# An attention-then-MLP kernel on one core: the list scheduler orders the same instructions by its timeline simulation instead of its core simulation

## The chip, the cores and the metric

The kernel runs on one core of a Trainium2 chip. The core has five engines that run side by side, each with its own instruction queue, executed strictly in the order in which the queue was written: TensorE (PE, matrix products, with a separate loader for weights, PEld), VectorE (DVE), ScalarE (ACT), GpSimd (POOL) and SyncE (SP, which here issues all the transfers). Engines wait for one another by semaphores. The metric is the device time of one execution in microseconds (us); smaller is better.

## The reference

Four batches of 12,480 tokens with 128 channels go through an attention by way of 32 inducing points, and then through an MLP with a squared ReLU:

```python
def mab(q, kv):
    s = scale * (q @ kv.transpose(0, 2, 1))
    a = np.exp(s - s.max(-1, keepdims=True))
    a /= a.sum(-1, keepdims=True) + 1e-09
    return a @ kv
h = mab(I, x)                 # (4, 32, 128): the inducing points attend to the tokens
y = mab(x, h)                 # (4, 12480, 128): the tokens attend to h
r = np.maximum(y.reshape(49920, 128) @ w_in, 0.0)      # w_in 128 x 2048
out = (r * r) @ w_out                                  # w_out 2048 x 128
```

## The kernel before

**Stages.** For each batch the kernel does four things.

- `first(b)`: the scores of the inducing points against the tokens (matmul s, L236, seven groups of up to 1920 tokens), their largest value (L254), the exponential on ACT (L300), a transpose on DVE (en, L310), and 28 pieces of the product with x accumulated in PSUM (hacc, L323) and added up (hq, L331). At the end stand hs (L336), hn (L340), ht (L343) and hT (L346), which is h of this batch, transposed. On the way DVE finds the largest magnitude of x per group (xm, L292, 128 x 1920).
- `prepare(b)`: a chain of small steps that turns h and the weights into this batch's constants. Since a token's attention weights over the 32 points add up to one, the MLP is rewritten as a quadratic form in those weights. The chain is hwv (L448), maxima (L463 to L479), a broadcast (bc, L482, and two, L484), scalings, hwS (L520), R (L529), pl (L537), rb (L560), cat (L578), w4 (L596), and then four times: DVE builds a tile G of products (L605, four instructions of 128 x 512; L607 once), PE multiplies it by w_out (wq, L611, 16 matmuls), and the result is written to the weights w16. G has one buffer, so that the next G waits for the wq before.
- `second(b, G)`: the attention of the tokens to h in seven groups of four chunks (s, L236; e, L362 to L375; the result goes out to DRAM as ad, L389, and comes back in another layout as dT, L409). `squares(b, G)` adds rows to dT (sq, L422; z, L428; zz, L432 on POOL; a transfer, L434).
- The chunks: 26 per batch, 104 in all, of 480 tokens. A chunk has two **ups** (`Chunk.up`, L639: two matmuls into hp, a tile of two PSUM banks, of which there are two), two **lifts** (`Chunk.lift`, L648: ACT squares hp into g, 128 x 960; three buffers of g), and a **down** (`Chunk.down`: four matmuls L654 with w16 and one L655 with lin into po, two buffers; then o, L658 on ACT or L660 on DVE, three buffers; then a transfer of o out, L661).

**What sets the order.** The code gives the instructions in one order: for each chunk n, the lift of half j, the up of half j of chunk n+1, and after the first half the down of chunk n-1; behind each half `background` gives some steps of the next groups' `second` and `squares` and of the next batch's `first` and `prepare`. This is the order in which the code is written, not the one that runs. `tile.TileContext` holds a list scheduler: it takes the instructions as they were given, keeps what depends on what, simulates the engines with a model of how long each instruction takes, and writes each engine's queue in the order in which the instructions became ready and were picked in that simulation. It chooses no other instructions and no other buffer sizes. A few places are tied by hand, with `tc.issue_after` (what stands in it comes behind the instruction that is named).

```python
    for n, chunk in enumerate(chunks):
        ...
        for j in (0, 1):
            chunk.lift(j)
            if nxt:
                nxt.up(j)
            if j == 0 and n:
                chunks[n - 1].down()
            k += 1
            background(k)
```

**The start.** Before any chunk, DVE splits the two weight matrices, which arrive as 64-bit words, into parts that it can compute with (`narrow`, L206 to L212, for w_in, seven instructions for each of four pieces wi; the same for w_out), works through a block of small constants (fold, rep, slot, late, cut, pairs, singles: L80 to L135), and does `first(0)`. wo_m (L186) and wo_b (L189) belong to the preparation of w_out; behind them PE does the hwv of batch 0.

At the very end of the program stands a branch for inputs on which the quadratic form isn't exact enough; it isn't taken here and costs the branch alone.

## Time and profile before

| | us |
|---|---|
| Three runs | 576.62, 576.66, 575.87; median 576.62 |
| The profiled execution: span, which is its own time | 577.3 |
| PE busy (in the span) | 438.9 (76%) |
| DVE busy | 365.3 (63%) |
| ACT busy | 296.8 (51%) |
| POOL busy | 83.4 (14%) |
| All transfers: 100.82 MB | 175 GB/s in the mean |

The profile page gives, for one execution, the busy time of each engine, the span in 40 equal slices with a digit for the busy share, the granted clock of TensorE in the same slices, and the chain of work that ended last. In the rows of a timeline stand the start in us, the duration in us, the engine, the line of the kernel, the operation, output<-input with shapes, and the count; in brackets what the engine waited for ahead of it. The rows of a waits view read: engine, line <- engine and line waited for, then us in total, times, the longest. The rows of a windows view read: window, its length, then busy us (and count) of PE, PEld, DVE, ACT, POOL, then the granted clock, the share of the DMA engines and GB/s.

The profiled span is 0.7 us above the median of the runs.

### The profile page before, as it was taken

What the parts mean: (1) busy time and instruction counts of PE and PEld (TensorE: products, weight loads), DVE (VectorE), ACT (ScalarE), POOL (GpSimd) and SP (SyncE); (2) the same over time, 40 slices, a digit from 0 to 9 for tenths busy, and PEclk for the clock granted to TensorE, in tenths of its full rate; (3) what the DMA queues carried; (4) which work ended last, traced back from release to release, by engine and by line L of the source; (5) the groups of instructions that cost most, each with busy time, mean ns of one, the idle gap of its engine ahead of it and who ended that gap; (6) DMA issues with size and microseconds to landing.
All of it is one profiled execution on the core that took longest, in us unless ns stands there. A gap on an engine that the chain in (4) does not pass through costs nothing.

```text
span 577.3 us, 8820 instructions
## 1 busy us (share of the span) xinstructions
PE 438.9 (76%) x3083; PEld 204.5 (35%) x3083; DVE 365.3 (63%) x947; ACT 296.8 (51%) x419; POOL 83.4 (14%) x93
## 2 busy tenths in 40 slices
PE   1615465777798889769878899769777999897882
PEld 0014334522233536413333545313243555223330
DVE  6999758662555268997254298985534378767342
ACT  0030112437577266747875376628574476565771
POOL 0000011030211010242021021222011022422010
PEclk9999655997789569989889799969969599899997
DMA  8958715024528606565867535735866332334543
GB/s 322 399 214 277 277 69 154 1 86 155 179 80 305 199 20 226 172 182 167 280 226 230 178 102 186 270 104 145 311 211 190 107 105 72 97 126 130 168 132 131
DMA packets 64590, 100.82 MB, mean 175 GB/s; under 512 B 22800, under 2 KB 53776, under 8 KB 64528
## 3 DMA queue, kind: packets, MB, share of 16 engines
q1 hardware_dynamic: 64528, 100.08, 52.1%
q8 instruction: 28, 0.46, 0.3%
q14 instruction: 34, 0.28, 0.2%
HBM read 64.91 MB, written 31.95 MB: 168 GB/s over the span
## 4 chain that ended last, share of the span: by engine, by line
PE 44%; DVE 28%; ACT 13%; issue 6%; DMA 3%; POOL 3%; SPq 1%; POOLq 0%; ACTq 0%; DVEq 0%
PE po L654 10%; PE hp L639 9%; ACT g L648 8%; PE s L236 7%; DVE xm L292 5%; PE hwv L448 5%; PE hacc L323 4%; DVE G L605 3%; DMA outT_dram<-o 2%; PE po L655 2%; PE wq L611 2%; ACT o L658 2%; DVE e L362 2%; PE R L529 2%; DVE z L372 2%
## 5 line engine op out<-in xcount | busy, mean ns | idle before, releaser
L648 ACT ACTIVATE g<-hp 128x960 f16<-128x960 f32 x208 | 193.2, 970 | 87.9 <-PE hp L639 48.9
L639 PE MATMUL hp<-dT,pairs 96*128 96x480 f16 x416 | 122.0, 385 | 29.0 <-ACT g L648 28.1
L654 PE MATMUL po<-g,w 128*128 128x480 f16 x416 | 119.4, 399 | 16.1 <-ACT o L658 6.0
L368 POOL TENSOR_TENSOR e<-e,mx 128x480 f32<-128x480 f32 (+1 forms) x28 | 26.5, 947 | 334.8 <-DVE mx L364 222.8
L639 PEld LDWEIGHTS <-pairs 96*128 96x128 f16 x416 | 37.8, 99 | 97.6 <-issue 75.7
L654 PEld LDWEIGHTS <-w 128*128 128x128 f16 x416 | 41.1, 104 | 75.4 <-issue 43.9
L292 DVE TENSOR_REDUCE xm<-xp_False 128x1 f32<-128x1920 f32 (+1 forms) x28 | 55.7, 1989 | 5.3 <-DMA xp_False<-xT_dram 5.3
L658 ACT ACTIVATE o<-po,bias,osc 128x480 f32<-128x480 f32 x66 | 48.9, 753 | 18.9 <-PE po L655 7.1
L236 PE MATMUL s<-xp_False,indT_sb 128*32 128x480 f32 (+1 forms) x224 | 37.7, 743 | 20.5 <-DMA xp_False<-xT_dram 12.3
L323 PE MATMUL hacc<-xnb,en 128*32 128x128 f32 x784 | 39.2, 328 | 17.2 <-issue 9.3
L655 PE MATMUL po<-dT,lin 128*128 128x480 f16 x104 | 42.3, 408 | 2.7 <-DMA dT<-zz 2.7
L432 POOL TENSOR_TENSOR zz<-z 128x480 f16<-128x480 f32 (+1 forms) x28 | 28.9, 1030 | 87.8 <-DVE z L428 72.1
L660 DVE TENSOR_SCALAR o<-po,osc,bias 128x480 f32<-128x480 f32 x38 | 28.7, 767 | 18.0 <-DMA outT_dram<-o 6.8
L323 PEld LDWEIGHTS hacc<-xnb,en 128*32 128x32 f32 x784 | 26.7, 129 | 34.3 <-issue 20.1
L300 ACT ACTIVATE sT<-sT,nb 128x480 f32<-128x480 f32 (+1 forms) x28 | 18.2, 653 | 35.5 <-DVE nb L287 35.5
L236 PE MATMUL s<-xp_False,hT 128*32 128x480 f32 (+1 forms) x224 | 34.5, 628 | 2.1 <-DVE s L357 1.7
L375 POOL TENSOR_TENSOR e<-e,z 128x480 f32<-128x480 f32 (+1 forms) x28 | 27.6, 986 | 53.8 <-DVE z L374 48.6
L428 DVE TENSOR_SCALAR z<-sq,off,cut 128x480 f32<-128x480 f32 (+1 forms) x28 | 21.4, 764 | 21.8 <-PE sq L422 21.7
L605 DVE TENSOR_TENSOR G<-hwp,hw 128x512 f16<-128x512 f16 x64 | 30.1, 510 | 5.0 <-PE wq L611 4.7
L369 ACT ACTIVATE e<-e 128x480 f32<-128x480 f32 (+1 forms) x28 | 16.1, 574 | 31.6 <-POOL e L368 31.6
L362 DVE STREAM_TRANSPOSE e<-s 128x480 f32<-128x480 f32 (+1 forms) x28 | 18.0, 644 | 15.4 <-PE s L236 14.9
L331 DVE TENSOR_TENSOR hq<-hacc,hq 128x128 f32<-128x128 f32 x24 | 6.8, 284 | 33.0 <-PE hacc L323 33.0
(208 smaller groups left out, 498.6 us busy)
## 6 DMA issues: line engine op xcount, KB each, us to landing
outT_dram<-o SPq DMA_DIRECT2D x104, 240.0 KB, 2.2
xp_False<-xT_dram SPq DMA_DIRECT2D x24, 960.0 KB, 5.8
xnb<-xn_dram SPq DMA_DIRECT2D x28, 448.0 KB, 6.1
xnb<-xn_dram SPq DMA_DIRECT2D x24, 512.0 KB, 5.8
dT<-ad SPq DMA_DIRECT2D x72, 120.0 KB, 2.7
ad<-a SPq DMA_DIRECT2D x24, 240.0 KB, 2.7
dT<-zz SPq DMA_DIRECT2D x104, 30.0 KB, 1.9
wi<-w_in_dram SPq DMA_DIRECT2D x4, 512.0 KB, 5.4
```

The costliest lines, as they stand in the source:

```text
L236: nc.tensor.matmul(ps[32 * q:32 * q + 32, 0:w], lhsT, xp[:, w * q:w * q + w], start=True, stop=True,)
L292: nc.vector.tensor_reduce(st.xm[:, G:G + 1], st.xp[G], axis=AX.X, op=ALU.max, apply_absolute_value=True,)
L323: st.last = nc.tensor.matmul(hacc[32 * q:32 * q + 32, 0:P], en[:, t], xg[:, t % 8], start=t < 4, stop=t + 4 >= nb32,)
L362: nc.vector.transpose(ef[:, 0:wb], ps[:, 0:wb])
L432: nc.gpsimd.tensor_tensor(g[rows], zv[rows], zv[rows], op=ALU.mult)
L448: nc.tensor.matmul(ps[:, k * (MI + 1):(k + 1) * (MI + 1)], w_in_sb[:, f:f + P], st.hT[:, 96:P + 1], start=True, stop=True,)
L605: tt(g[:, :, MI * j:MI * j + n], hwp[:, :, 0:n], hw16f[:, :, s0:s0 + n], op=ALU.mult)
L639: nc.tensor.matmul(hp[:, i, 0:CH].rearrange("p (q t) -> p q t", q=4), pairs[0:96, (2 * j + i) * P:(2 * j + i + 1) * P], self.dT[0:96], sta ...
L648: nc.scalar.activation(self.g[:, 2 * j:2 * j + 2], self.hp.pop(j)[:, 0:2, 0:CH], AF.Square)
L654: nc.tensor.matmul(po[:, 0:CH], st.w16[:, i], self.g[:, i], start=i == 0, stop=False)
L655: nc.tensor.matmul(po[:, 0:CH].rearrange("p (q t) -> p q t", q=4), st.lin, self.dT, start=False, stop=True)
L658: nc.scalar.activation(o, po[:, 0:CH], AF.Identity, bias=st.bias, scale=st.osc)
```

## The change

One argument of the tile context is added. The scheduler then runs its timeline simulation, in place of the default core simulation, to decide which instruction of those that are ready comes next on each engine.

```diff
-    with tile.TileContext(nc) as tc:
+    with tile.TileContext(nc, schedule_with_timeline_sim=True) as tc:
         attend_then_relu2_mlp(tc, *aps)
```

Every engine gets the same instructions as before; what moves is their order, on PE, DVE, ACT, POOL and SP alike, and with it where each waits. Three places are shown. In the rows stand the line, the operation and output<-input with a running number, and x for a repetition.

**DVE at the start.** ni0 and ni1 are the first two pieces of w_in being narrowed, out of the words wi0 and wi1; the rows on fold to singles are the block of small constants. Before:

```order
L563 MEMSET cat_0_686 32x16
L206 TENSOR_SCALAR ni0_a_193<-wi0_171 128x512
L207 SCALAR_TENSOR_TENSOR ni0_a_193<-wi0_171,ni0_a_193 128x512
...
L206 TENSOR_SCALAR ni1_a_203<-wi1_173 128x512
L212 SCALAR_TENSOR_TENSOR w_in_sb_128<-ni0_m_194,ni0_r_195 128x512
L80 TENSOR_REDUCE fold_84<-ident_74 128x32 x2
L82 COPY rep_87<-fold_84 128x128
...
L135 CAST singles1_149<-fold_84 64x16
L207 SCALAR_TENSOR_TENSOR ni1_a_203<-wi1_173,ni1_a_203 128x512
```

And now:

```order
L563 MEMSET cat_0_686 32x16
L80 TENSOR_REDUCE fold_84<-ident_74 128x32 x2
L93 TENSOR_REDUCE late_97<-ident_74 128x1
L82 COPY rep_87<-fold_84 128x128
...
L135 CAST singles1_149<-fold_84 64x16
L206 TENSOR_SCALAR ni0_a_193<-wi0_171 128x512
L207 SCALAR_TENSOR_TENSOR ni0_a_193<-wi0_171,ni0_a_193 128x512
...
L206 TENSOR_SCALAR ni1_a_203<-wi1_173 128x512
L212 SCALAR_TENSOR_TENSOR w_in_sb_128<-ni0_m_194,ni0_r_195 128x512
L207 SCALAR_TENSOR_TENSOR ni1_a_203<-wi1_173,ni1_a_203 128x512
```

The block from fold to singles has moved from behind the first piece to ahead of it, and so ahead of DVE's first wait for wi0.

**PE among the chunks.** hp_3_20_0 is the first half's up of chunk 20 of the last batch, po_3_19 the down of chunk 19. Each matmul has a row for the loading of its weights ahead of it, left out here, as are repetitions. Before:

```order
L639 MATMUL hp_3_20_0_5295<-dT_3_5_5106,pairs_109 128x480
...
L639 MATMUL hp_3_20_1_5308<-dT_3_5_5106,pairs_109 128x480
...
L655 MATMUL po_3_17_5280<-dT_3_4_4995,lin1_147 128x480
...
L655 MATMUL po_3_18_5298<-dT_3_4_4995,lin1_147 128x480
...
L639 MATMUL hp_3_21_0_5313<-dT_3_5_5106,pairs_109 128x480
...
L655 MATMUL po_3_19_5316<-dT_3_4_4995,lin1_147 128x480
```

And now:

```order
L639 MATMUL hp_3_20_0_5295<-dT_3_5_5106,pairs_109 128x480
...
L654 MATMUL po_3_19_5316<-g_3_19_5293,w16_1_146 128x480
...
L639 MATMUL hp_3_20_1_5308<-dT_3_5_5106,pairs_109 128x480
...
L654 MATMUL po_3_19_5316<-g_3_19_5293,w16_1_146 128x480
...
L655 MATMUL po_3_19_5316<-dT_3_4_4995,lin1_147 128x480
...
L639 MATMUL hp_3_21_0_5313<-dT_3_5_5106,pairs_109 128x480
```

Before, two ups in a row were followed by two whole downs in a row, and the ups ran up to four chunks ahead of the downs (2.8 in the mean over the program). Now one up (two matmuls) and half a down (two matmuls) alternate here, and the ups are 1.5 chunks ahead. The alternation stands in chunks 8 to 17 of the first and of the second batch, 8 to 21 of the third and 16 to 25 of the last; over the program the ups are 2.1 chunks ahead in the mean.

**PE at the end of a batch.** R_1, rb_1, w4_1 and wq_1 are steps of the preparation of batch 1, hp_0_24 and hp_0_25 the last ups of batch 0, and po_0_22 to po_0_25 its last downs, of which the last row of each is shown. Before:

```order
L529 MATMUL R_1_1763<-wo_sb_129,hwS_1_1740 32x128 x16
...
L639 MATMUL hp_0_24_0_2110<-dT_0_6_1634,pairs_109 128x480
...
L596 MATMUL w4_1_1876<-w_hi_130,g4_1_1800 32x128
...
L655 MATMUL po_0_22_2113<-dT_0_5_1404,lin0_136 128x480
...
L611 MATMUL wq_1_0_1928<-w_hi_130,G_1_0_1919 128x128
...
L655 MATMUL po_0_23_2141<-dT_0_5_1404,lin0_136 128x480
...
L611 MATMUL wq_1_1_1975<-w_hi_130,G_1_1_1947 128x128
...
L639 MATMUL hp_1_0_0_2178<-dT_1_0_1914,pairs_109 128x480
...
L611 MATMUL wq_1_3_2076<-w_hi_130,G_1_3_2051 128x128
```

And now:

```order
L639 MATMUL hp_0_24_0_2110<-dT_0_6_1634,pairs_109 128x480
...
L529 MATMUL R_1_1763<-wo_sb_129,hwS_1_1740 32x128 x16
...
L655 MATMUL po_0_22_2113<-dT_0_5_1404,lin0_136 128x480
...
L655 MATMUL po_0_23_2141<-dT_0_5_1404,lin0_136 128x480
...
L639 MATMUL hp_1_0_0_2178<-dT_1_0_1914,pairs_109 128x480
...
L596 MATMUL w4_1_1876<-w_hi_130,g4_1_1800 32x128
...
L611 MATMUL wq_1_0_1928<-w_hi_130,G_1_0_1919 128x128
...
L611 MATMUL wq_1_1_1975<-w_hi_130,G_1_1_1947 128x128
...
L611 MATMUL wq_1_3_2076<-w_hi_130,G_1_3_2051 128x128
```

The steps of the preparation have moved back against the chunks. Counted in chunks whose ups and downs stand ahead on PE (a half is one of two ups, or some of the matmuls of a down), R moves from (23, 20) to (25.5, 22), rb from (24, 22) to (26, 25.5), wq_0 from (24.75, 23) to (28, 26) and wq_3 from (28, 26) to (30, 26.75); the ends of the second and third batch read alike.

## The prediction, made before the changed kernel was run

> **What bounds the kernel now.** First the page: span, busy times, the strips of 40 slices (14.4 us each) and the chain that ended last.
>
> ```profile
> span 577.3 us, 8820 instructions
> PE 438.9 (76%) x3083; PEld 204.5 (35%) x3083; DVE 365.3 (63%) x947; ACT 296.8 (51%) x419; POOL 83.4 (14%) x93
> PE   1615465777798889769878899769777999897882
> DVE  6999758662555268997254298985534378767342
> ACT  0030112437577266747875376628574476565771
> PEclk9999655997789569989889799969969599899997
> PE 44%; DVE 28%; ACT 13%; issue 6%; DMA 3%; POOL 3%; SPq 1%; POOLq 0%; ACTq 0%; DVEq 0%
> ```
>
> Three regimes. In slices 2 to 4 DVE is full and PE mostly idle: everything waits for DVE. From about the eighth slice PE is at 7 to 9 tenths to the end, and no other engine is full for long. PE is then the bound, but with gaps: those, and not its work, are what another order can change. So next the windows, cut at each batch's head and end.
>
> ```profile
> 128.00:194.00 66.00, 53.07 (x387) 19.98 (x385) 30.04 (x65) 44.60 (x66) 10.93 (x12) 0.82 0.53 171
> 194.00:255.00 61.00, 51.90 (x356) 29.03 (x360) 46.13 (x133) 35.55 (x51) 10.05 (x10) 0.86 0.52 169
> 255.00:315.00 60.00, 49.85 (x378) 18.46 (x375) 29.69 (x66) 40.88 (x60) 10.08 (x11) 0.89 0.68 219
> 315.00:378.00 63.00, 53.09 (x393) 29.32 (x392) 47.08 (x138) 36.37 (x51) 10.18 (x10) 0.92 0.57 183
> 378.00:440.00 62.00, 51.69 (x380) 20.04 (x377) 35.18 (x73) 36.12 (x52) 9.45 (x10) 0.83 0.62 201
> 440.00:500.00 60.00, 54.98 (x383) 29.80 (x383) 37.58 (x132) 36.49 (x52) 10.52 (x10) 0.89 0.30 98
> 500.00:568.00 68.00, 56.84 (x255) 21.20 (x254) 38.43 (x67) 42.62 (x49) 13.54 (x15) 0.95 0.44 144
> ```
>
> After the length come PE's busy time and those of PEld, DVE, ACT and POOL, then the clock. PE is idle for 68.6 us of the 440 (440 - 371.4, the sum of the column), about equally everywhere: 12.9, 9.1, 10.2, 9.9, 10.3, 5.0 and 11.2 us. So every stage has a gap to win and another can lose one. What ends PE's idle time is in its waits (us, times, longest), the first two over the span, the last two in the window 500 to 570; below them is the lift's row of the page, with ACT's idle time before it:
>
> ```profile
> PE hp L639 <- ACT g L648: 28.1, 56, 2.8
> PE wq L611 <- DVE G L605: 3.1, 4, 1.4
> PE po L654 <- DVE o L660: 5.1, 8, 1.7
> PE hp L639 <- ACT g L648: 3.7, 10, 0.7
> ...
> L648 ACT ACTIVATE g<-hp 128x960 f16<-128x960 f32 x208 | 193.2, 970 | 87.9 <-PE hp L639 48.9
> ```
>
> Mostly an up waits until ACT has lifted the hp two halves earlier. The two engines take turns over two buffers, and ACT has 87.9 us of its own idle time before L648: a rhythm in which each waits for the other, and which the order sets.
>
> **The change, part by part.** No instruction is added or removed, so the sum has only terms of moved work. Against the span they are four.
>
> *(1) The start: -3.2 us.*
>
> ```profile
> 4.93 0.43 DVE L206 TENSOR_SCALAR ni_a<-wi 128x512 uint32<-128x512 uint32 x1 [3.52 <-DMA wi<-w_in_dram]
> 9.19 0.63 DVE L80 TENSOR_REDUCE fold<-ident 128x32 f32<-128x128 f32 x2
> 12.07 0.67 DVE L207 SCALAR_TENSOR_TENSOR ni_a<-wi,ni_a 128x512 uint32<-128x512 uint32 x1
> 69.46 3.63 PE L448 MATMUL hwv<-hT,w_in_sb 128*128 128x33 f32 x16
> 83.11 2.13 DVE L292 TENSOR_REDUCE xm<-xp_False 128x1 f32<-128x1920 f32 x1
> xp_False<-xT_dram SPq DMA_DIRECT2D x24, 960.0 KB, 5.8
> ```
>
> DVE sits idle for 3.52 us before the first word of w_in lands at 4.93. The block of constants takes 12.07 - 9.19 = 2.88 us after it. Now the block comes first and fits into the wait; DVE is saturated until about 68 us and hands the 2.88 on. I estimate 0.3 us more from reduces of x no longer standing between hs and hn, so that hwv starts near 66.1 instead of 69.46. Against it: the third xm of batch 1 and an element-wise group of `second` now stand ahead of the maxima of hwv, and that xm waits for a transfer (5.8 us to landing) issued only when an x buffer comes free; in return the xm at 83.11 (2.13 us) is no longer in the chain before R. I let these two cancel. Bounds: -1 (the transfer's wait eats all but one) and -4.5 (the chain loses the 2.13 and pays half of it elsewhere). I take -3.2, since the 2.88 is measured directly and nothing on DVE replaces it.
>
> *(2) The last twenty chunks: -5 us.* They have neither a next batch nor a preparation beside them, so they show the rhythm alone.
>
> ```profile
> 541.16 0.97 PE L654 MATMUL po<-g,w 128*128 128x480 f16 x4
> 541.97 0.37 PE L655 MATMUL po<-dT,lin 128*128 128x480 f16 x1
> 541.22 2.70 ACT L648 ACTIVATE g<-hp 128x960 f16<-128x960 f32 x3 [1.84 <-PE po L654]
> 551.73 2.69 ACT L648 ACTIVATE g<-hp 128x960 f16<-128x960 f32 x3 [1.84 <-PE po L654]
> 561.18 2.70 ACT L648 ACTIVATE g<-hp 128x960 f16<-128x960 f32 x3 [1.89 <-PE po L654]
> 554.77 4.52 ACT L648 ACTIVATE g<-hp 128x960 f16<-128x960 f32 x5 [0.35 <-PE hp L639]
> 535.00:568.00 33.00, 27.54 (x128) 11.22 (x125) 13.41 (x20) 22.48 (x25) 2.95 (x3) 1.00 0.48 163
> ```
>
> The same pattern, ACT waiting 1.84 us while PE does two downs in a row, returns at 541.22, 551.73 and 561.18, each time after four chunks: (561.18 - 541.22) / 8 = 2.49 us a chunk. The floors are lower. PE has nine matmuls (four ups, five of the down); four start within 541.97 - 541.16 = 0.81 us, so 0.20 each and 1.83 in all. ACT has two lifts of 4.52 / 5 = 0.90, so 1.81 (and a third of the o's). Neither floor is 2.49: the difference is the turn-taking. With one up and half a down in alternation, ACT lifts one hp (0.90) while PE does half a down and the next up (4.5 x 0.20 = 0.91), and nobody waits for two downs. I take 2.25 a chunk, under half of the way to the floor, since o, its buffers and the transfers out still wait (5.1 us here): 20 x (2.49 - 2.25) = 4.8, say -5. Bounds: 0, if PE still waits for each lift because only two hp exist, and -8.4, if all of PE's idle time goes (33 - 27.54 = 5.46 us over 13 chunks, 0.42 a chunk, twenty times).
>
> *(3) The alternating chunks of the first three batches: -4.5 us.* Ten, ten and fourteen. The up's wait for the lift is 28.1 - 3.7 = 24.4 us outside the tail, over 78 chunks, 0.31 a chunk; all of it over 34 chunks would be -10.6. The granted clock is 0.82 to 0.89 there and `first(b+1)` runs beside, so PE's own work is longer and the waits are less its bound: under half, -4.5. The other bound is +5: the preparation of the next batch starts late (hs of batch 1 behind 18 downs instead of 16), two chunks at 2.49.
>
> *(4) The ends of the three batches: +5 us.* Here the change takes cover away.
>
> ```profile
> 224.24 1.19 PE L560 MATMUL rb<-hot,hws 128*32 128x16 f32 x32
> 229.08 1.06 PE L611 MATMUL wq<-w_hi,G 128*128 128x128 f16 x16
> 238.11 1.07 PE L611 MATMUL wq<-w_hi,G 128*128 128x128 f16 x16 [1.35 <-DVE G L605]
> 241.80 1.07 PE L611 MATMUL wq<-w_hi,G 128*128 128x128 f16 x16 [0.74 <-DVE G L607]
> L605 DVE TENSOR_TENSOR G<-hwp,hw 128x512 f16<-128x512 f16 x64 | 30.1, 510 | 5.0 <-PE wq L611 4.7
> ```
>
> From the first wq to the last pass 12.7 us (241.80 - 229.08). DVE needs 4 x 0.51 for a G and PE 1.07 for the wq, one after the other because G has one buffer: three rounds are at least 3 x 3.1 = 9.3. Before, PE did three downs and 3.25 chunks of ups meanwhile. Now it has three quarters of a down and two chunks of ups: (0.75 x 5 + 2 x 4) x 0.20 = 2.4 us, plus three wq, 3.2: 5.6 in 9.3 to 12.7. That leaves 3.7 to 7.1 us idle, against 2.1 in the rows above (1.35 + 0.74): 1.6 to 5 a batch, 5 to 15 in all, unless `second` and `squares`, in the gaps, fill them. The downs that no longer cover were done earlier, so work is not added, but a batch can't start its downs before the last wq. I take the lower end, +5, since matmuls of the next batch's `second` stand there too; bounds 0 and +15.
>
> Sum: -3.2 - 5 - 4.5 + 5 = -7.7. Span 577.3 - 7.7 = 569.6. The profiled execution is 0.7 above the median of the runs (576.62), so **568.9 us**.
>
> **The rivals.**
>
> *The last wq decides.* The place is the G and wq chain at the three ends; the price is the upper 15 us of (4). For it: R, rb, cat and wq all move back by two to four chunks, and PE waited there even with the cover. Against: ups and `second` go on. It decides once it costs over 12.7, the sum of the gains. With +15 and the heads at their bad end (+5, which is the same lateness), and the start and tail as forecast: 577.3 - 3.2 - 5 + 5 + 15 - 0.7 = 588.4; with the heads at zero 583.4. I call it 585.
>
> *The clock falls.* Alternation leaves many short idles on PE. In the trace the clock is 1.00 from 535 to 568 in spite of them, but 0.82 to 0.92 in the batches, and low where PE is seldom busy:
>
> ```profile
> 93.16 6.13 PE L529 MATMUL R<-wo_sb,hwS 128*32 128x128 f32 x32 [7.53 <-DVE hwS L520]
> 467.82 3.68 PE L529 MATMUL R<-wo_sb,hwS 128*32 128x128 f32 x32
> ```
>
> The same 32 matmuls take 6.13 us after 7.53 idle, and 3.68 in a busy stretch: a factor of 1.67. A chunk's 1.83 would become 3.05 and be the bound: 20 x (3.05 - 2.49) = +11 in the tail instead of -5, and -3.2 - 4.5 + 5 beside it: 584.9. [...]
>
> *More than forecast.* Heads at -10, tail at -7, start -3.2, ends +2: 577.3 - 18.2 - 0.7 = 558.4. For it: over 60 us of PE idle time to be had.
>
> *The start alone.* Alternation is worth nothing because hp has two buffers either way, and the ends cost nothing: 577.3 - 3.2 - 0.7 = 573.4.
>
> *Gains and losses cancel,* or the waits only move from one line to another: 576.
>
> **How the numbers follow.** Forecast 0.39 (its own range 562 to 573); more 0.12; the start alone 0.12; cancel 0.09; last wq 0.20; clock 0.08. A measurement of this kernel tells 0.2%, 1.2 us, from no change, so the first three are faster (0.63), the fourth the same (0.09), the last two slower (0.28). The range, 8 in 10: the lower end 554, below the rival with more; the upper end 586, past most of the first rival and the clock's.
>
> **What would show it.** (1) right: first L206 still near 4.9 with the block before it, first hwv near 66; wrong: hwv earlier but R no earlier. (2) right: in the last twenty chunks ACT's waits of 1.84 for po are gone and four chunks take about 9 us; wrong: still 10, with hp waiting for g. (3) right: hp's wait for g falls by more than 5 us between 128 and 500. (4) wrong: over 5 us of PE waiting for G per batch end, or the first L655 of a batch late by it. The clock: under 0.9 in the tail. The forecast is wrong if the gains of (2) and (3) return as waits at the ends, or if the chunks' time does not follow the order of ups and downs at all.

## The result and the profile after

The changed kernel takes 558.55 us in the median of four runs (553.92 to 565.03), the kernel before 576.64; the ratio is 0.965 (95% interval 0.959 to 0.970), 18 us less. In a second comparison it was 557.5 against 577.4, 0.967 (0.961 to 0.974). The prediction said 568.9, 7.7 us less: the sign is right and the time lies in the stated range, but the forecast is less than half of the measured change. Times here and below are medians over all runs, while the ratios leave out runs that lay over 1.5% above the fastest of their kernel, so the two can differ by some us. The lines below come from a profile of the second comparison (span 554.5 us); the first profile, of an execution that took 565.0 us, is named where it differs.

The page of the changed kernel, in the form shown of before:

```profile
span 554.5 us, 8828 instructions
PE 416.4 (75%) x3083; PEld 200.5 (36%) x3083; DVE 366.1 (66%) x947; ACT 294.3 (53%) x419; POOL 82.0 (15%) x93
PE   1535356876878889769789978769789989688892
PEclk9657556998789889788889798777899989889997
PE 37%; DMA 27%; DVE 19%; issue 6%; SPq 4%; ACT 4%; POOL 1%; ACTq 0%; DVEq 0%; POOLq 0%
```

No engine does less: the counts are the same, and DVE, ACT and POOL are busy as long as before. On the chain that ended last, transfers (DMA) have 27% where they had 3%. PE's busy time is 22.5 us shorter for the same 3083 matmuls, and its idle time, the span less the busy time, is what it was: 138.4 us before, 138.1 now. Read literally, the whole gain is in busy time and none in gaps. The count is the same, so this isn't work saved; and a matmul's row can run on past the start of the next (before, four from 541.16 have 0.97 us, and the next starts at 541.97), so the two can't be told apart by it.

The granted clock is part of the question: its mean is 0.85 against 0.87, but only because of the first 115 us (about 0.70, an estimate from the first eight digits of its strip, against 0.84, with PE idle for half of it); from batch 0's last wq to batch 3's it is 0.89 against 0.87 (0.88, 0.87 and 0.91 in the three batches, before 0.84, 0.90 and 0.86). How much of the shorter busy time is the clock, no run separates; over the 19 runs of the kernel before in the second comparison the mean clock went from 0.84 to 0.91 without a visible relation to the time (572.2 us at 0.89, 580.5 at 0.90).

The places are read better from marks in the timeline. A batch's preparation ends with its fourth wq, which opens its downs; so the time from one fourth wq to the next is what a batch costs. In the timeline of PE, before (start, us, engine and line):

```profile
114.92 1.07 PE L611 MATMUL wq<-w_hi,G 128*128 128x128 f16 x16 [0.79 <-DVE G L607]
241.80 1.07 PE L611 MATMUL wq<-w_hi,G 128*128 128x128 f16 x16 [0.74 <-DVE G L607]
365.60 1.07 PE L611 MATMUL wq<-w_hi,G 128*128 128x128 f16 x16 [0.54 <-DVE G L607]
490.31 1.06 PE L611 MATMUL wq<-w_hi,G 128*128 128x128 f16 x16
...
499.29 0.36 PE L655 MATMUL po<-dT,lin 128*128 128x480 f16 x1 [0.53 <-DMA dT<-zz]
522.14 0.37 PE L655 MATMUL po<-dT,lin 128*128 128x480 f16 x1
567.14 0.37 PE L655 MATMUL po<-dT,lin 128*128 128x480 f16 x1
```

And in the changed kernel:

```profile
110.01 1.07 PE L611 MATMUL wq<-w_hi,G 128*128 128x128 f16 x16 [0.59 <-DVE G L607]
236.02 1.45 PE L611 MATMUL wq<-w_hi,G 128*128 128x128 f16 x16
359.44 1.89 PE L611 MATMUL wq<-w_hi,G 128*128 128x128 f16 x16 [0.32 <-DVE G L607]
475.15 1.37 PE L611 MATMUL wq<-w_hi,G 128*128 128x128 f16 x16 [0.22 <-DVE G L607]
...
487.34 0.57 PE L655 MATMUL po<-dT,lin 128*128 128x480 f16 x2
499.73 0.37 PE L655 MATMUL po<-dT,lin 128*128 128x480 f16 x1
543.33 0.36 PE L655 MATMUL po<-dT,lin 128*128 128x480 f16 x1
```

The three L655 rows are the downs of chunks 78 (the first of the last batch), 85 and 103. Worked out from the differences, with two more profiles of the same order beside them (the first one of the changed kernel, and the run of Set 4 that ties all five queues to this order, but for a few rows of the start):

| stage | before | changed | difference | first profile | all tied |
|---|---|---|---|---|---|
| start, to batch 0's last wq | 114.9 | 110.0 | -4.9 | 114.7 | 110.1 |
| batch 0, to batch 1's last wq | 126.9 | 126.0 | -0.9 | 128.5 | 126.2 |
| batch 1 | 123.8 | 123.4 | -0.4 | 121.8 | 118.5 |
| batch 2 | 124.7 | 115.7 | -9.0 | 116.3 | 113.7 |
| last batch, to its last down | 76.8 | 68.2 | -8.6 | 70.8 | 73.0 |
| of it to the down of chunk 78 | 9.0 | 12.2 | +3.2 | 12.2 | 15.2 |
| of it chunks 78 to 85 | 22.9 | 12.4 | -10.5 | 11.3 | 10.5 |
| of it chunks 85 to 103 | 45.0 | 43.6 | -1.4 | 47.3 | 47.3 |

So the same order differs by up to 5 us a stage from one execution to the next; the gain in batch 2 and the last batch stands in all three. The last three rows depend on the mark: between the downs of chunks 85 and 86 the changed kernel puts ups and half downs of later chunks (8.8 us, 2.1 before), and counted from chunk 86 the rest of the last batch takes 34.8 us against 42.9.

The waits of PE for what follows, before (in us, times, the longest):

```profile
PE sq L422 <- DMA dT<-ad: 7.2, 2, 3.7
PE po L655 <- DMA dT<-zz: 2.7, 4, 1.5
```

And the first four in the changed kernel:

```profile
PE s L236 <- DMA xp_False<-xT_dram: 15.0, 5, 11.6
PE sq L422 <- DMA dT<-ad: 13.9, 8, 4.0
PE po L655 <- DMA dT<-zz: 9.2, 7, 1.9
PE hp L639 <- ACT g L648: 8.6, 16, 1.2
```

The up's wait for the lift is down from 28.1 us to 8.6. In its place PE waits for transfers: dT<-ad from 7.2 to 13.9, dT<-zz from 2.7 to 9.2. So waits moved to transfers, all of which SP issues, and SP's own waits, which the prediction had not looked at, changed much too. Before:

```profile
SPq L434 <- POOL zz L432: 81.8, 22, 8.3
SPq L661 <- ACT o L658: 50.1, 18, 7.7
SPq L267 <- PE hacc L323: 36.4, 17, 8.6
```

And in the changed kernel:

```profile
SPq L231 <- PE s L236: 77.7, 11, 17.0
SPq L434 <- POOL zz L432: 49.8, 16, 11.6
SPq L661 <- ACT o L658: 43.2, 27, 5.3
```

Before, SP's queue stood 82 us with a transfer dT<-zz at its head that POOL had not made ready, and whatever came behind it stood too. In the changed kernel it stands 77.7 us at loads of x (L231) that wait for PE instead (45 us before, for s and sq), and its waits in sum are hardly shorter: all rows of the view add up to 341 us before and 323 now. So the length of the waits alone doesn't say what the order changes; what stands behind them, the view doesn't show. SP's timeline before, near the end, shows an example:

```profile
548.16 0.57 SPq L389 DMA_DIRECT2D ad<-a  x1
551.07 0.60 SPq L434 DMA_DIRECT2D dT<-zz  x1
551.76 0.54 SPq L661 DMA_DIRECT2D outT_dram<-o  x1
552.35 0.58 SPq L434 DMA_DIRECT2D dT<-zz  x1
553.04 1.50 SPq L409 DMA_DIRECT2D dT<-ad  x3
554.58 1.24 SPq L434 DMA_DIRECT2D dT<-zz  x2
555.92 1.51 SPq L661 DMA_DIRECT2D outT_dram<-o  x3
```

SP issues nothing from 548.7 to 551.07; then a transfer dT<-zz and one out, and three more outs only at 555.92, behind the transfers of dT. Each issue takes it 0.50 to 0.62 us in these rows. What such a place costs PE isn't in these rows.

### The profile page after: what moved, and what is told of

Read it like the earlier page. It is cut to its first block, busy times and chain, and to the rows that moved or that the text cites. A ratio compares the mean times of both kernels' runs of the same rounds, so it can differ in the third digit from the quotient of the medians.

```text
span 563.2 us, 8828 instructions
## 1 busy us (share of the span) xinstructions
PE 422.6 (75%) x3083; PEld 202.7 (36%) x3083; DVE 365.6 (65%) x947; ACT 294.4 (52%) x419; POOL 82.2 (15%) x93
## 4 chain that ended last, share of the span: by engine, by line
PE 39%; DMA 24%; DVE 22%; ACT 5%; SPq 4%; issue 3%; POOL 0%; ACTq 0%; DVEq 0%; POOLq 0%
PE hp L639 11%; DMA dT<-ad 7%; PE po L654 6%; PE s L236 6%; DMA xp_False<-xT_dram 6%; DMA ad<-a 5%; DVE xm L292 5%; ACT g L648 4%; DMA xnb<-xn_dram 3%; PE wq L611 3%; DVE G L605 3%; PE hwv L448 3%; PE hacc L323 2%; SPq L409 2%; DMA outT_dram<-o 2%
## 5 line engine op out<-in xcount | busy, mean ns | idle before, releaser
L639 PE MATMUL hp<-dT,pairs 96*128 96x480 f16 x416 | 129.3, 407 | 16.2 <-ACT g L648 9.6
L654 PE MATMUL po<-g,w 128*128 128x480 f16 x416 | 114.7, 381 | 13.0 <-DVE o L660 5.1
L323 PE MATMUL hacc<-xnb,en 128*32 128x128 f32 x784 | 35.6, 317 | 19.6 <-DMA xnb<-xn_dram 7.6
L655 PE MATMUL po<-dT,lin 128*128 128x480 f16 x104 | 39.9, 400 | 9.3 <-DMA dT<-zz 9.0
L432 POOL TENSOR_TENSOR zz<-z 128x480 f16<-128x480 f32 (+1 forms) x28 | 27.6, 985 | 111.7 <-DVE z L428 87.9
L660 DVE TENSOR_SCALAR o<-po,osc,bias 128x480 f32<-128x480 f32 x38 | 28.8, 763 | 18.4 <-PE po L655 13.7
L323 PEld LDWEIGHTS hacc<-xnb,en 128*32 128x32 f32 x784 | 25.5, 125 | 32.5 <-issue 15.7
L236 PE MATMUL s<-xp_False,hT 128*32 128x480 f32 (+1 forms) x224 | 30.0, 610 | 0.1
L605 DVE TENSOR_TENSOR G<-hwp,hw 128x512 f16<-128x512 f16 x64 | 25.9, 460 | 5.6 <-PE wq L611 5.6
L378 DVE STREAM_TRANSPOSE a<-e 128x480 f32<-128x480 f32 (+1 forms) x28 | 17.7, 633 | 13.0 <-POOL e L375 13.0
L422 PE MATMUL sq<-dT,singles 96*32 96x480 f16 x104 | 11.4, 398 | 19.4 <-DMA dT<-ad 18.0
```

Of the source, the lines that this page charges most:

```text
L236: nc.tensor.matmul(ps[32 * q:32 * q + 32, 0:w], lhsT, xp[:, w * q:w * q + w], start=True, stop=True,)
L323: st.last = nc.tensor.matmul(hacc[32 * q:32 * q + 32, 0:P], en[:, t], xg[:, t % 8], start=t < 4, stop=t + 4 >= nb32,)
L432: nc.gpsimd.tensor_tensor(g[rows], zv[rows], zv[rows], op=ALU.mult)
L605: tt(g[:, :, MI * j:MI * j + n], hwp[:, :, 0:n], hw16f[:, :, s0:s0 + n], op=ALU.mult)
L639: nc.tensor.matmul(hp[:, i, 0:CH].rearrange("p (q t) -> p q t", q=4), pairs[0:96, (2 * j + i) * P:(2 * j + i + 1) * P], self.dT[0:96], sta ...
L654: nc.tensor.matmul(po[:, 0:CH], st.w16[:, i], self.g[:, i], start=i == 0, stop=False)
```

## Experiments

In most of them the order of some instructions is tied: a list of instructions of one engine is queued in that order, by edges that order the issue and add no wait; the scheduler places the rest around them. The helper, once:

```diff
+def pin(tc, nc, orders):
+    traced = {i.name: i for i in nc.cur_bb.bb.instructions}
+    for seq in orders:                       # numbers of one engine's instructions
+        for a, z in zip(seq, seq[1:]):
+            tc.add_manual_dep(traced[f"I-{z}"], f"I-{a}", mybir.DependencyInfo(
+                mybir.DependencyClass.NoSync, mybir.DependencyReason.DATA), reason="pin")
...
+    pin(tc, nc, ORDERS)                      # behind the last chunk
     short = const.tile([1, 1], I32, name="short")
```

Each diff below says what ORDERS holds and which scheduler places the rest. Ratios are to the kernel before, with the 95% interval.

**Set 1: the parts that the prediction priced, put into the kernel before.**

```diff
 # the changed kernel, once more
```

> The changed kernel once more, for a second profile, since its runs so far lie 11 us apart (553.9 to 565.0) where those of before lie within 2. Both theories: 554 to 565 us. Theory A (the order of ups and downs on PE makes the gain): the up's wait for the lift stays near 10 us against 28.1 before, in this execution too. Theory B (the gain lies in the other queues, which start the next batch's scores and preparation earlier): the last wq of batch 3 stays some 9 us earlier than before (481 against 490).

```diff
+ORDERS = [PE of the changed kernel, all 2234 matmuls]        # scheduler of before
```

> The scheduler of before, with all 2234 matmuls of PE queued in the order of the changed kernel; the other engines are ordered by the scheduler of before around that. Theory A (PE's order makes the gain): 555 to 563 us. Theory B (the orders of DVE, ACT and SP make it): 572 to 577.

```diff
+ORDERS = [PE: L639, L654, L655 in the changed order]         # scheduler of before
```

> The scheduler of before, with only the 936 matmuls of ups and downs queued in the changed kernel's order among themselves; where the preparation and the scores stand between them is free. Theory A as forecast (the rhythm gains, the ends of the batches lose): 560 to 565 us, since the preparation's steps may stand earlier again. If it is PE's order but the place of the preparation in it that counts: 570 to 577. Theory B: 572 to 577.

```diff
+ORDERS = [DVE: fold ... singles (L80 to L135), then the first L206]   # scheduler of before
```

> The scheduler of before, with DVE's block of small constants queued ahead of the first narrowing, as in the changed kernel; nothing else is tied. The forecast's first term: hwv starts near 66.5 instead of 69.46 and the run ends 3.2 us earlier, 573.4. Rival: the gain at the start is lost before the first chunk is done (its L655 ended at 127.8 with the change and 127.9 before), 576.6.

Measured: the changed kernel again 557.5; PE's whole queue 602.3 (1.036, 1.027 to 1.046); ups and downs alone 579.9 (1.003, 0.998 to 1.007); the start alone 580.7 (1.005, 1.001 to 1.008). None of the parts that were put in gains anything by itself, and PE's order by itself loses 21 us by the ratio and 25 by the medians, more than either theory allowed (555 to 577). Theory A, which the forecast rests on, falls in this form. With PE's queue of the changed kernel the waits of PE for o rise from 6.0 and 5.7 us to

```profile
PE po L654 <- ACT o L658: 16.4, 11, 3.4
PE po L654 <- DVE o L660: 12.6, 6, 5.0
```

as it seems because ACT, DVE and SP do not bring their o's when PE now expects them. The start alone is a miss of its own: with the block of constants ahead of the first narrowing, hwv began not 3 us earlier but 1.6 later. But it isn't a test of the start alone: around the tied rows the scheduler moved the first xm into the middle of the first narrowing, and DVE stood 5.12 us there, waiting for x:

```profile
11.82 2.15 DVE L292 TENSOR_REDUCE xm<-xp_False 128x1 f32<-128x1920 f32 x1 [5.12 <-DMA xp_False<-xT_dram]
71.03 3.63 PE L448 MATMUL hwv<-hT,w_in_sb 128*128 128x33 f32 x16
```

**Set 2: the chunks' rhythm against everything else.**

```diff
+ORDERS = [PE, ACT, DVE, SP: L639, L648, L654, L655, L658, L660, L661, changed order]   # scheduler of before
```

> The scheduler of before, with the chunks' own instructions (ups, downs, lifts, o and its transfer out) queued in the changed kernel's order among themselves on PE, ACT, DVE and SP; everything else is free. With PE's ups and downs alone tied, the waits of PE for o rose from 11.7 to 24 us, so this run ties the engines that answer PE as well. Theory A (the rhythm of the chunks over all engines makes the gain): 557 to 566 us. Theory B (where the next batch's first pass and preparation stand makes it): 574 to 580.

```diff
+ORDERS = [all five engines: everything but those lines, changed order]   # scheduler of before
```

> The scheduler of before, with everything but the chunks' own instructions queued in the changed kernel's order among itself on all five engines (start, first pass, preparation, second, squares); the chunks are free. Theory A: 573 to 580 us. Theory B: 558 to 566. If both are needed together: 570 to 576.

```diff
+ORDERS = [PE, ACT, DVE, SP: those lines in the order of before]   # changed scheduler
```

> The changed kernel's scheduler, with the chunks' own instructions queued in the order of before among themselves on PE, ACT, DVE and SP. Theory A: the gain is gone, 572 to 580 us. Theory B: the gain stays, 555 to 562.

```diff
+ORDERS = [DVE: the first narrowing, then the constants, as before]   # changed scheduler
```

> The changed kernel's scheduler, with DVE's block of small constants queued behind the first narrowing again, as before. If the start's gain counts at the end of the changed kernel (its last wq of batch 0 came 4.9 us earlier in the second profile, 110.0 against 114.9): 560.5 to 562.5 us against 557.5. If it is lost later or the block isn't what made it: 556 to 559.

Measured: the rhythm alone 583.3 (1.005, 1.001 to 1.009); the background alone 588.2 (1.017, 1.010 to 1.023); the changed kernel with the rhythm of before 548.4 (0.942, 0.931 to 0.952); with the start of before 562.7 (0.972, 0.965 to 0.979). The first two lie above, and the third below, everything that was expected of them. So neither half of the order carries the gain into the other's surroundings. The third run decides on the rhythm: taking the new rhythm away doesn't lose the gain, it adds 9 us to it by the medians (15 by the ratios). The up's wait for the lift doesn't follow the rhythm either: with the new rhythm under the scheduler of before, and with the old one under the changed scheduler, it is

```profile
PE hp L639 <- ACT g L648: 33.2, 35, 7.8
PE hp L639 <- ACT g L648: 14.0, 31, 1.4
```

against 28.1 before and 8.6 in the changed kernel. The last wq's of the third run:

```profile
110.38 1.07 PE L611 MATMUL wq<-w_hi,G 128*128 128x128 f16 x16 [0.59 <-DVE G L607]
231.41 1.06 PE L611 MATMUL wq<-w_hi,G 128*128 128x128 f16 x16
345.78 1.06 PE L611 MATMUL wq<-w_hi,G 128*128 128x128 f16 x16
457.48 1.07 PE L611 MATMUL wq<-w_hi,G 128*128 128x128 f16 x16 [0.54 <-DVE G L607]
```

Its batches take 121.0, 114.4 and 111.7 us, 5.0, 9.0 and 4.0 less than in the changed kernel; its last batch 78.5 us (to a last down at 535.98), 10.3 more. Against the two other profiles of the changed order the signs are the same, with 2 to 8 us a batch and 5.5 to 7.7 in the last. So the chunks' new order costs where a next batch is prepared beside the chunks, and gains in the last batch, where nothing is. The scheduler placed the rest around the tied rows, so that the surroundings aren't quite those of the changed kernel. The start's 5 us by the medians (562.7 against 557.5; 3 by the ratios) are of the size expected, but the two intervals overlap.

**Set 3: do the stages add up, and which queue carries the rest?**

```diff
+ORDERS = [PE, ACT, DVE, SP: the rhythm of before for chunks 0 to 77]   # changed scheduler
```

> The changed kernel's scheduler, with the chunks of the first three batches (0 to 77) in the rhythm of before and the last batch left to the scheduler. From the last wq of a batch to the next, the profiles show: with the rhythm of before throughout 121.0, 114.4, 111.7 and 78.8 us to the end of the chunks; the changed kernel 126.0, 123.4, 115.7 and 68.6. If the stages add up: 548.4 - (78.8 - 68.6) = 538 us. If the last batch's gain hangs on what the batch before leaves behind: 546 to 550.

```diff
+ORDERS = [the rhythm of before; PE: also s1, mt, mb, hacc, hs, ht of batches 1 to 3 as before]   # changed scheduler
```

> As the run with the rhythm of before under the changed scheduler (548.4), but on PE the first pass of the next batch (s1, mt, mb, hacc, hs, ht of batches 1 to 3) is queued where it stood among the ups and downs before: two to four chunks later in the second and third batch (mt of batch 2 behind 37 downs instead of 33, hs behind 42 instead of 38). Theory C (an earlier place of the next batch's chain makes the gain): 566 to 577 us. Theory D (the place doesn't matter; it is that the queues of the five engines fit one another): 545 to 552.

```diff
+ORDERS = [PE, DVE, ACT, POOL whole, changed order; SP free]   # scheduler of before
```

> The scheduler of before, with PE, DVE, ACT and POOL queued wholly in the changed kernel's order; only SP's queue, which issues all transfers, is ordered by the scheduler of before around them. If SP's order carries the gain: 570 to 600 us (PE's order alone gave 602). If it carries none: 555 to 561, as the changed kernel.

```diff
+ORDERS = [PE, ACT, SP whole, changed order; DVE and POOL free]   # scheduler of before
```

> The scheduler of before, with PE, ACT and SP queued wholly in the changed kernel's order; DVE and POOL are ordered by the scheduler of before around them. If DVE's order carries the gain (the loss of 602 with PE alone came from DVE's steps standing too late for PE's): 570 to 600 us. If it carries none: 555 to 561.

Measured: 541.4 (0.936, 0.930 to 0.943), by the median the fastest version of the study, 2.9% under the changed kernel's 557.5, though not clear of the run with the old rhythm throughout (0.931 to 0.952); 608.9 (1.057, 1.053 to 1.061); 589.2 (1.019, 1.014 to 1.024); 569.2 (0.987, 0.983 to 0.991). The stages add up (541 against 538): the last batch takes 66.8 us in place of 78.5. In its alternating chunks the downs follow one another at PE's floor, here the rows of two of them in its timeline:

```profile
522.99 0.36 PE L655 MATMUL po<-dT,lin 128*128 128x480 f16 x1
524.82 0.36 PE L655 MATMUL po<-dT,lin 128*128 128x480 f16 x1
```

1.83 us a chunk, as worked out from nine matmuls of 0.20. Its windows view has a clock of 1.00 over that batch (the columns as in the prediction):

```profile
461.20:528.30 67.10, 61.85 (x337) 26.22 (x337) 47.09 (x86) 54.98 (x64) 16.55 (x17) 1.00 0.52 170
```

A later place for the first pass costs far more than either theory said (60 us instead of 20 to 30): the place matters, but the other queues moved with it, so that its price isn't isolated by this run. The two runs with queues left free say where the changed order is needed: against the changed kernel's 557.5, leaving DVE and POOL to the scheduler of before costs 12 us, and leaving SP to it 32.

**Set 4: which transfers on SP, with a control.**

```diff
+ORDERS = [all five engines whole, changed order]   # scheduler of before
```

> A control: the scheduler of before, with all five queues tied to the changed kernel's order (SP, PE and ACT are then the same, DVE and POOL differ in a few rows of the start). If the order is all that the scheduler's model changes: 554 to 562 us, as the changed kernel. If tying by itself costs time, or the scheduler changes something else: over 566, and the runs with tied queues would have to be read anew.

```diff
+ORDERS = [PE, DVE, ACT, POOL whole; SP: L231, L267 to L271, L197, L661, changed order]   # scheduler of before
```

> As the run with all queues but SP's tied (589.2), and on SP the loads of x and the transfers of o out in the changed kernel's order among themselves; the way of the attention's result (ad, dT, zz) is free. Theory S1 (loads of x that stand behind transfers of o, which wait for ACT, hold up the next batch's first pass): 555 to 563 us. Theory S2 (it is the result's way out to DRAM and back): 580 to 592.

```diff
+ORDERS = [PE, DVE, ACT, POOL whole; SP: L389, L409, L434, L661, changed order]   # scheduler of before
```

> As the run with all queues but SP's tied (589.2), and on SP the way of the attention's result (ad, dT, zz) and the transfers of o out in the changed kernel's order among themselves; the loads of x are free. Theory S1: 578 to 592 us. Theory S2: 555 to 565.

```diff
+ORDERS = [PE, DVE, ACT, POOL whole; SP: all but L661, changed order]   # scheduler of before
```

> As the run with all queues but SP's tied (589.2), and on SP everything but the transfers of o out in the changed kernel's order. If it is the transfers of o that stand ahead of others and wait for ACT (SP waited 69.7 us for ACT's o there, 43.2 in the changed kernel): 575 to 590 us. If the order of loads against ad, dT and zz is what counts: 555 to 563.

Measured: all tied 556.9 (0.967, 0.962 to 0.973), which is the changed kernel: its order is the whole of its effect, and tying costs nothing. Of SP's 32 us, loads and outs tied give back nothing and cost 11 more (600.3; 1.039, 1.035 to 1.044), the attention's way and the outs tied give 22.5 (566.7; 0.982, 0.977 to 0.986), everything but the outs 14.5 (574.7; 0.993, 0.989 to 0.997). So S2 is borne out in its direction, if not in its ranges (580 to 592, and 555 to 565): most of it is how ad, dT and zz stand against the outs, and the last 10 us come with the loads. SP's waits, with its queue free, with loads and outs tied, and with the attention's way and outs tied:

```profile
SPq L661 <- ACT o L658: 69.7, 38, 6.8
SPq L434 <- POOL zz L432: 60.7, 23, 11.6
```

```profile
SPq L434 <- POOL zz L432: 76.4, 23, 13.1
SPq L661 <- ACT o L658: 63.4, 30, 8.3
```

```profile
SPq L661 <- ACT o L658: 48.6, 30, 5.7
SPq L434 <- POOL zz L432: 48.2, 14, 11.6
```

589.2, 600.3 and 566.7 us go with 60.7, 76.4 and 48.2 us at zz, and the fourth run, 574.7, with 57.5. But the wait isn't the whole of it: the run with all queues tied has 50.5 us at zz and takes 556.9, 10 less than the one with 48.2, and the background alone (Set 2) has 40.7 and takes 588.2.

**Set 5: the transfers that wait longest, off SP's queue.**

```diff
-            nc.sync.dma_start(dT[96:P, :, j * TP:(j + 1) * TP], g[MI * j:MI * j + MI])
+            nc.gpsimd.dma_start(dT[96:P, :, j * TP:(j + 1) * TP], g[MI * j:MI * j + MI])
```

> The kernel before, with the 104 transfers dT<-zz issued by POOL, which computes zz, in place of SP. SP's queue stood 81.8 us at these transfers before (22 times, longest 8.3) with whatever came behind them, and 49.8 in the changed kernel; over the runs with the changed kernel's rhythm the time rose with it (48.2 us: 566.7; 60.7: 589.2; 76.4: 600.3). Theory Z (a wait at the head of SP's queue, and what is held behind it, is what the order changes): 560 to 570 us. Rival (the wait is harmless, since nothing that PE needs soon stands behind it): 573 to 580.

> The changed kernel, with the same transfers issued by POOL. Theory Z: a smaller gain than the kernel before has from it, 550 to 556 us, since less wait at the head of the queue is left. Rival: 555 to 561, no change.

Measured: the kernel before falls to 548.7 (0.950, 0.943 to 0.956), the changed kernel to 552.5 (0.955, 0.947 to 0.963). The first is what theory Z foresaw, and more (560 to 570 had been expected); the second lies in its range, but its 5 us against the changed kernel are not clear of it (0.961 to 0.974). Without these transfers on SP the default scheduler is 30 us faster and the timeline simulation has no advantage left. Waits of PE in the kernel before with this edit:

```profile
PE po L655 <- DMA dT<-zz: 16.1, 10, 4.7
PE hp L639 <- ACT g L648: 13.7, 22, 2.0
```

The up's wait for the lift, which the prediction took for a rhythm between PE and ACT, halves (28.1 to 13.7) with no rhythm asked for. Two limits. The scheduler also placed other instructions anew once POOL issues these transfers (the next batch's first mt stands behind 9 downs instead of 12), so the run doesn't part the queue without zz from the new places. And SP's queue doesn't wait less: it stands 104 us for ACT's o (50 before), and its waits add up to 388 us (341 before). So that a shorter wait at the head makes the gain isn't shown; that taking zz off SP under this scheduler gains 5% is.

## Why the prediction was right or wrong

- **The step that failed** is "a rhythm in which each waits for the other, and which the order sets", and with it the sum, which took the gain from the places of ups, downs and preparation on PE and had no term for SP, DVE or POOL after the start. The new rhythm under the scheduler of before gained nothing (583.3 us, and the up's wait at 33.2); the old one under the changed scheduler kept the gain and more (548.4, with the wait at 14.0). In the place of the rhythm stand the other engines' queues: with PE, DVE, ACT and POOL in the changed order, SP's order alone is worth 32 us, and DVE's and POOL's 12. Every transfer goes through SP's one queue (425 issues in the trace of before), which stood 82 us at one line before.
- **The views read** were PE's and ACT's waits. That the gaps of PE, "and not its work, are what another order can change", isn't borne out by the page: the up's wait fell by 19.5 us, others grew, and PE's idle time is the same (138.4 and 138.1).
- **(1) The start, -3.2:** hwv began at 66.5 us (67.2 in the first profile) against 69.5, about as forecast (66.1; its own terms give 66.3). The block did fit into the wait for wi (it starts at 1.5 us, L206 still at 5.0). At the last wq of batch 0 this is -4.9 in one profile and -0.2 in the first, with the same order: the granted clock was 0.9 or more in the one (the strip's slice from 97.0 to 110.9 us) and 0.54 in the other (100 to 110 us). Putting the block back in the changed kernel moved hwv by 2.4 us (to 68.8) and cost 3 to 5 us, with overlapping intervals.
- **(2) The last twenty chunks, -5:** the mechanism is right and the size is within its bounds. ACT's waits for po are gone, and in most of the alternating chunks the downs follow at 1.83 us, below the 2.25 taken. From chunk 86 to 103 it is -8.1 us in the changed kernel's profile and -6.6 in the run with all queues tied; but counted from chunk 85, -1.4 and +2.3.
- **(3) and (4), -4.5 and +5:** this is the mis-sized part. Together they said +0.5; the three batches gave -10.3 (-0.9, -0.4, -9.0). Both signs were right and both sizes far off: from the down of a batch's chunk 8 to that of its chunk 18 the three batches took 59.7, 57.4 and 60.6 us before and 48.5, 39.8 and 37.5 in the changed kernel, 52 less, beyond the bound of -10.6; the rest of the three batches lost 42 of it, because a later down is not a later batch. What counts is when the next batch's preparation ends, and that hangs on the whole chain, transfers included. With the old rhythm under the changed scheduler the three batches took 347 us, against 375 before and 365 in the changed kernel: what surrounds the chunks gained 28, and their new order cost 18 of it. The sum had the second, near nothing, and not the first.
- **Rivals:** the last wq did not decide, and the clock did not fall as that rival has it: over the last batch it was 0.95 in the changed kernel, against 0.96 before, and 1.00 in the fastest version; from chunk 85's down to the end it was 0.93 in the first profile, against 1.00 before, all above the 0.9 that was named for it. Nor is the clock low wherever PE is seldom busy, as the prediction reads it: before, it was 1.00 in the first 57.7 us, with PE busy for 22.0 of them, and 0.57 from there to 101 us, with PE busy for 23.5 of 43.3. The number of "more than forecast" (558.4) was met, but by luck: its cause, a larger gain of the same rhythm, isn't what the runs show.

What stays open: how much of SP's 32 us is standing at zz and how much the place of what is behind it, since no run moved the one without the other; why the chunks' new order costs inside the batches; and why PE's busy time, and not its idle time, got shorter.

## What to carry to other kernels

When the change moves order on every engine, price every queue, the one that issues transfers above all: read its own waits, and ask what stands behind each. An order is worth something only together with the other engines' orders: pieces of a good schedule put into another lost up to 4%. And where transfers wait long at the head of a queue, try issuing them from another engine: here that was worth 9 us more than the change of schedule.

## What had not been expected of the hardware

The same program, executed again, spread over 11 us (553.9 to 565.0), where the runs of before that stood beside it lay within 2; but in the second comparison it was 2.4 us, against 8.2 for 19 runs of before, so the spread isn't a mark of the schedule. One stretch of it is seen: in the same order, batch 0's last wq came at 110.0 us or at 114.7, with a granted clock of 0.9 or more from 97.0 to 110.9 us in the one and 0.54 from 100 to 110 us in the other. Also, 104 small transfers issued by POOL took 558 ns of that engine each and 3.1 us to land, against 1.9 us when SP issued them, and the kernel was still 5% faster:

```profile
L434 POOL DMA_DIRECT2D dT<-zz x104 | 57.4, 558 | 7.7 <-POOL zz L432 5.3 <-PE hp L639 1.5 <-DMA dT<-ad 0.9
dT<-zz POOLq DMA_DIRECT2D x104, 30.0 KB, 3.1
```
